# Attention and two expert layers in one kernel: the early weight chunks and the coefficients get other places in the order of issue

## The chip, the cores and the metric

The kernel runs on one core of one Trainium2 chip. The metric is the device time of one launch in microseconds; lower is better.

## The reference

```python
scores = scale * q @ k.T                       # 4 batches, 8 heads, 576 rows, 64 wide
scores = where(scores >= max(scores) - tau, scores, -1e9)
x = softmax(scores) @ v                        # then heads side by side: 2304 x 512
h = x @ w_in                                   # 512 x 2048, float64 weights
P = a[0] + a[1]*h + a[2]*h**2 + a[3]*h**3
Q = 1 + abs(b[0])*abs(h) + abs(b[1])*h**2
x = (P / (Q + 1e-6)) @ w_out                   # 2048 x 512, float64 weights
e = argmax(x @ w_gate, axis=1)                 # top-1 of 8 experts
out[rows of e] = gate_w * sigmoid(x @ w_output_gate)[e] * (relu(x @ w1[e]) @ w2[e])
```

## The kernel before

Every instruction is issued by a hand-written order; each engine takes its own in that order and waits on semaphores.

*Attention.* `attention` runs 144 steps, 18 to a group of four heads, N = 144. A step makes one block of scores on TensorE (`emit_s`, L356). VectorE takes the row minimum (L367) and masks (L380), ScalarE takes the exponential (L368) and writes the high half of the probabilities (L384), GpSimd the low half (L386, L392). Every two steps SP issues a DMA transpose of that pair (L394), out of a ring of four buffers. The product with v (`emit_pv`, L414) follows twelve steps later (LAG). After six such products VectorE normalises: a reciprocal and a multiplication (`emit_x`, L424, L425). The next product writes the same PSUM tile and waits for it. `emit_xt` turns normalised rows into xT (TensorE L206, ScalarE L445), `emit_xlo` makes the low half (VectorE L451). Pieces of the next group's queries and keys and of v are put into `plan`, by step.

*The second stage beside it.* `moe1` is a generator. The loop enters it once per step in the last 33 steps (`next(tail)` where `i >= N - PRE`), so its slot t stands at step 112 + t. Its first entry issues the loads of the coefficients a and b on SP (L678, L679); `coefficients` (L681) then negates and takes absolute values on VectorE and ScalarE. Slots hold lists of functions (`at`, `run`).

*Weight chunks.* w_in and w_out come as 32 raw chunks of 512 KB in the order of `STREAM`, (0, n) for w_in and (1, n) for w_out, through five buffers. `IN_LOAD` gives the slots of the first seven loads (L610); later ones are issued when a chunk has been decoded. A chunk is decoded from its float64 bits by ScalarE (`exponent`, L622) and three VectorE passes (`bits` L619, `merge` L625, `sign` L629). The first two chunks have their passes at the slots of `EARLY_STEPS`, the next six at `FIRST_AT`. `sum_in` (ScalarE, L801) sums absolute values; per two chunks `red_in` adds the rows on TensorE (L810) in a `tp` tile, `clamp_red` and `scale_in` (L635 to L654) make a power of two on VectorE, `split_in` splits the scaled chunk into two halves on ScalarE and GpSimd (L847, L848, L852).

*Chunks of the second stage.* From slot START on, `emit_in(c)` multiplies one chunk of w_in with three tiles of rows (L947). At odd c it issues, for that pair, three ScalarE passes (L970 to L972), a GpSimd product (L973) and two VectorE passes (L975, L976); for the pair before, three more VectorE passes (L961 to L963), whose result feeds `emit_out` (L1016), five chunks behind. Slot 34 is cut into three (`HALVES`): the second row sum, its scale and the first of its splits come between the last products of the attention, which are issued after the loop, one part at a time, between entries of the generator.

Of the kernel before, what the change touches and what calls it, by code (L numbers as in the profile page):

```python
# [49 lines left out]
MAG_BUFS = 4  # L50
MAG2_BUFS = 6
PART_BUFS = 3
PRE = 32
END = 37
START = 33
G_LAG = 5
FILL = (0, 0, 9, 0, 0)
IN_LOAD = (0, 3, 13, 17, 21, 32, 32)
STREAM = ((0, 0), (0, 1), (0, 2), (0, 3), (1, 0), (1, 1), (1, 2), (1, 3), (0, 4), (0, 5), (0, 6), (0, 7), (1, 4), (1, 5), (1, 6), (1, 7), (0, 8), (0, 9), (0, 10), (0, 11), (1, 8), (1, 9), (0, 12), (0, 13), (1, 10), (1, 11), (0, 14), (0, 15), (1, 12), (1, 13), (1, 14), (1, 15))
EARLY_STEPS = ((9, 11, 13), (15, 17, 19))  # L60
EARLY_SUM = 20
FIRST_AT = (13, 19, 32, 33, 35, 37, 37, 38)
SHIFT_LEAD = 3
SLOT_LEAD = (2, 1)
SECOND_SUM = 34
HALVES = (34,)
DEC_AT = 39
DEC_EVERY = 1.6


# [65 lines left out]
def attention(nc, tc, q, k, v, tau, xT, vs, ident, tail, bank):  # L136
# [260 lines left out]
    def emit_pv(i):  # L397
        g, hh, t = step(i)
        par = g % 2
        pt = pairs[i // 2]  # L400
        k = UT * (i % 2)
        if i % 6 == 0:

            nc.tensor.matmul(xflat, tiny[:, 0:P], tiny[:, P:], start=True, stop=False)
        b_hi, b_lo = (k + 5, k) if hh else (k, k + 5)
        parts = ((0, P, 0),) if t < 4 else ((0, 64, 0), (64, 64, 1)) if t == 4 else ((0, P, 1),)
        for po, m, bb in parts:
            rows = [4 * bb + (j + 2 * hh) % 4 for j in range(4)]
            seq = [(b_hi + j, vv, r) for j, r in enumerate(rows) for vv in (vh, vl)]
            seq += [(k + 4, vv, 8 + bb) for vv in (vh, vl)]  # L410
            seq += [(b_lo + j, vh, r) for j, r in enumerate(rows)]
            x = xps[po:po + m, i % 6, :]
            for n, (blk, vv, j) in enumerate(seq):
                nc.tensor.matmul(  # L414
                    x, pt[:, blk, po:po + m], vv[:, par, hh, j, :], start=False, stop=(i % 6 == 5 and n == 13))
# [3 lines left out]
    def emit_x(n):  # L419
        g, m = divmod(n, 3)  # L420
        if m == 0:
            xfs[g] = x_p.tile([P, GT, D], F32, tag="xf", name="xf")
        rs = sm.tile([P, 6, 1], F32, tag="rinv", name="rinv")
        nc.vector.reciprocal(rs, xps[:, :, D:D1])  # L424
        nc.vector.tensor_tensor(  # L425
            xfs[g][:, 6 * m:6 * m + 6], xps[:, :, 0:D], rs.to_broadcast([P, 6, D]), op=ALU.mult)
# [8 lines left out]
    def emit_xt(g, tg, k=None, what=None):  # L435
        if (g, tg) == (NG - 1, 2):
            tp = xflat[:, 0:3 * P].rearrange("p (a b) -> p a b", b=P)
        else:
            tp = ps_x.tile([P, 4, P], F32, tag="tp", name="tp")
        if what:  # L440
            piece_t(k, what, tp=tp, n=3)
        for t in range(3):
            for hh in range(2):
                turn(tp[:, t], hh, xfs[g][:, UT * hh + 3 * tg + t], ident)
        nc.scalar.activation(x_rows(g, tg, 0), tp[:, 0:3], AF.Copy)  # L445
        if what:
            piece_out(k, what)
        xts[g, tg] = tp
# [42 lines left out]
    def at(step, f, *a):  # L491
        plan.setdefault(step, []).append((f, a))
# [43 lines left out]
    pre = {6 * n + 6 + LAG: n for n in range(N // 6 - 2)}  # L536
    for g in range(NG):
        for tg in range(3):
            s = min((g + 1) * GT + PLAN["xt"][tg], N)
            if g == NG - 1:  # L540
                continue
            w = (g + 2, (("kt",), ("qt", 0), ("qt", 1))[tg]) if g + 2 < NG else ()
            at(s, emit_xt, g, tg, *w)
            at(min(s + 1, N), emit_xlo, g, tg)
    emit_s(0)
    for i in range(N + 1):
        if i + 1 < N:
# [21 lines left out]
    next(tail)  # L569
    for i in range(N - LAG, N - 6):  # L570
        emit_pv(i)
    next(tail)
    emit_x(N // 6 - 2)
    for i in range(N - 6, N - 4):
        emit_pv(i)
    next(tail)
    for i in range(N - 4, N - 2):
        emit_pv(i)
    emit_xt(NG - 1, 0)
    emit_xlo(NG - 1, 0)  # L580
    next(tail)
    for i in range(N - 2, N):
        emit_pv(i)
    emit_x(N // 6 - 1)
# [83 lines left out]
def moe1(nc, tc, xT, vs, w_in, w_out, a, bb, w_gate, w_ogate, gates, ident, yd, part, L, consts, keep, side, early_bank):  # L668
# [43 lines left out]
    def at(slot, f, *args):  # L712
        hooks.setdefault(max(slot, 0), []).append((f, args))
# [143 lines left out]
        nc.scalar.activation(h, f, AF.Copy)  # L857
        nc.gpsimd.tensor_tensor(l, f, h.bitcast(F32), op=ALU.subtract)  # L858

    at(1, coefficients)  # L860
    end = decode_at()
    for key in STREAM:
        t = end[key]
        if key in STREAM[:2]:
            for x, f in zip(EARLY_STEPS[STREAM.index(key)], step_parts(key)):
                steps.setdefault(x, []).append(f)
            t = EARLY_STEPS[STREAM.index(key)][0]
        else:
            steps.setdefault(t, []).append(lambda key=key: step(key))
        at(t - SLOT_LEAD[late(key)], exponent, key)  # L870
        if late(key) and key[0]:
            at(t - SHIFT_LEAD, last_bits, key)
    n = 0
    for m in GROUPS:
        if n < 2 * m:
            for i in range(n, n + m):
                at(end[0, i] + (n == 0), sum_in, i)
            t = SECOND_SUM if n else EARLY_SUM + 1
            at(t + 0.5, red_in, n, m, True)
            at(t + 0.75, clamp_red, n, m)  # L880
            at(t + 0.75, scale_in, n, m)
            for i in range(m):
                at(t + (0.8, 1)[i] if n else t + 2 + 2 * i, split_in, n + i)
            at(t + 1, factors_in, n, m)
        else:
            for i in range(n, n + m):
                at(end[0, i] + 1, sum_in, i)
            t = max(end[0, i] for i in range(n, n + m)) + 1
            at(t + 1, red_in, n, m)
            at(t + SC_LAG, scale_in, n, m)  # L890
            at(t + SC_LAG, factors_in, n, m)
            for i in range(m):
                at(t + IN_LAG + i * SPLIT2, split_in, n + i)
        n += m
# [40 lines left out]
    def emit_in(c, fill):  # L935

        p, odd = divmod(c, 2)
        ops, late = [], []
        if c < len(chunks):
            j, fc, r = chunks[c]  # L940
            t0 = TR * r
            if not odd:
                hps[p] = h_tile()
            hb = hps[p][:, odd]
            parts = [(0, k, lo) for k in range(4) for lo in range(2)] + [(1, k, 0) for k in range(4)]
            for i, (w, k, lo) in enumerate(parts):
                nc.tensor.matmul(  # L947
                    hb[:, 0:n], w_cols(w, fc)[:, k], xT[:, k, t0:t0 + TR, lo, :],
                    start=(i == 0), stop=(i == 11))
            if spare:  # L950
                first, last = spare.pop(0)(hb[:, n:DM])
                if first:
                    first()
                late.append(last)
        if odd:
            if p - 1 in st:
                q = p - 1
                t, s = st.pop(q)
                x = hps.pop(q)[:, :, 0:n]
                ops += [  # L960
                    lambda: stt(t, t, one, x, op0=ALU.add, op1=ALU.mult),  # L961
                    lambda: stt(x, t, 2.0, x, op0=ALU.subtract, op1=ALU.mult),
                    lambda: (stt(s, s, na0, x, op0=ALU.add, op1=ALU.mult), emit_g(q, s)),  # L963
                ]
            if c < len(chunks):

                hp = hps[p][:, :, 0:n]
                c1, c2, ca1, ca3 = (cvs[:, i, t0 // UT, fc - 1:fc] for i in range(4))
                ah, t1, s1 = buf("ah", 1), buf("t", 3), buf("s", 4)
                nc.scalar.activation(ah, hp, AF.Abs, scale=c1)  # L970
                nc.scalar.activation(s1, hp, AF.Identity, bias=na2, scale=ca3)
                nc.scalar.activation(t1, ah, AF.Identity, bias=b0, scale=b1)  # L972
                nc.gpsimd.tensor_tensor(t1, t1, ah, op=ALU.mult)  # L973
                ops += [
                    lambda: stt(s1, s1, c2, hp, op0=ALU.mult, op1=ALU.mult),  # L975
                    lambda: stt(s1, s1, ca1, hp, op0=ALU.add, op1=ALU.mult),  # L976
                ]
                st[p] = t1, s1
        elif p - 1 in st:

            x, t = hps[p - 1][:, :, 0:n], st[p - 1][0]
            nc.scalar.activation(x, t, AF.Ln, bias=one)  # L982
            nc.scalar.activation(x, x, AF.Exp, scale=-1.0)
        ops += late
        fill = list(fill)
        for f, k in itertools.zip_longest(ops, FILL):
            if f:
                f()
            for _ in range(min(k or 0, len(fill))):
                fill.pop(0)()  # L990
        for f in fill:
            f()
# [896 lines left out]
```

## Time and profile before

| | us |
|---|---|
| median of 3 runs | 1029.98 (1028.72 to 1033.62) |
| profiled execution | 1033.16 |
| its span, first to last instruction | 1031.4 |
| TensorE busy | 934.7 (91%) |
| VectorE busy | 797.6 (77%) |
| ScalarE busy | 680.4 (66%) |
| GpSimd busy | 542.5 (53%) |

The attention loop fills the first 312 us or so, the second stage with the expert layers the rest. In the rows PE is TensorE and PEld its weight loads, DVE is VectorE, ACT ScalarE, POOL GpSimd, SP SyncE, and SPq SP's issue of DMAs. Times are counted from the span's start. A bracket at the end of a row tells how long the engine stood idle before it, and what ended that.

### The profile page before, as it was taken

What the parts mean: (1) busy time and instruction counts of PE and PEld (TensorE: products, weight loads), DVE (VectorE), ACT (ScalarE), POOL (GpSimd) and SP (SyncE); (2) the same over time, 40 slices, a digit from 0 to 9 for tenths busy, and PEclk for the clock granted to TensorE, in tenths of its full rate; (3) what the DMA queues carried; (4) which work ended last, traced back from release to release, by engine and by line L of the source; (5) the groups of instructions that cost most, each with busy time, mean ns of one, the idle gap of its engine ahead of it and who ended that gap; (6) DMA issues with size and microseconds to landing.
All of it is one profiled execution on the core that took longest, in us unless ns stands there. A gap on an engine that the chain in (4) does not pass through costs nothing. (4 is left out here: it accounts for less than half of the span.)

```text
span 1031.4 us, 20730 instructions
## 1 busy us (share of the span) xinstructions
PE 934.7 (91%) x7899; PEld 685.4 (66%) x7899; DVE 797.6 (77%) x1337; ACT 680.4 (66%) x1006; POOL 542.5 (53%) x540
## 2 busy tenths in 40 slices
PE   8898899996977799999899999998798999999996
PEld 5565566664655465666566666665477899999995
DVE  5897799985996897888767878898983896656552
ACT  5888888885885687788756666665462555545552
POOL 2687689885793569687964444444241131111120
PEclk9999999998998899999999999999899999999998
DMA  9999999998998233223003213032123011111340
GB/s 211 175 203 204 197 190 188 185 198 158 163 194 181 81 106 131 82 92 113 1 1 82 72 31 93 2 92 89 55 52 131 23 52 52 42 42 42 108 138 24
DMA packets 234188, 110.26 MB, mean 107 GB/s; under 512 B 196832, under 2 KB 221408, under 8 KB 234080
## 3 DMA queue, kind: packets, MB, share of 16 engines
q1 hardware_dynamic: 230816, 98.89, 44.3%
q0 software_dynamic: 3120, 9.96, 3.0%
q8 instruction: 64, 1.05, 0.4%
q14 instruction: 44, 0.36, 0.1%
q10 hardware_dynamic: 144, 0.00, 0.0%
HBM read 82.61 MB, written 13.63 MB: 93 GB/s over the span
## 5 line engine op out<-in xcount | busy, mean ns | idle before, releaser
L386 POOL TENSOR_TENSOR php<-e,php 128x512 f16<-128x512 f32 x144 | 166.5, 1160 | 73.8 <-ACT php L384 73.5
L973 POOL TENSOR_TENSOR t<-t,ah 128x768 f32<-128x768 f32 x48 | 88.3, 1839 | 176.3 <-ACT t L972 169.8
L947 PE MATMUL h<-xT,wih 128*128 128x384 f16 x768 | 145.0, 333 | 34.5 <-DVE s L963 22.4
L947 PEld LDWEIGHTS <-wih 128*128 128x128 f16 x768 | 68.8, 99 | 99.4 <-DVE s L963 28.2
L368 ACT ACTIVATE e<-s,mn 128x576 f32<-128x576 f32 x144 | 107.1, 744 | 32.9 <-DVE mn L367 29.7
L1016 PE MATMUL acc<-woh,gh 128*128 128x512 f32 x288 | 126.2, 438 | 2.9 <-ACT woh L857 1.6
L414 PEld LDWEIGHTS <-pt 128*128 128x128 f16 (+1 forms) x2240 | 79.7, 102 | 67.7 <-issue 55.4
L356 PE MATMUL s<-kt,qT 64*128 64x256 f32 (+3 forms) x640 | 116.1, 452 | 8.3 <-DVE mn L373 7.6
L380 DVE SCALAR_TENSOR_TENSOR e<-s,mn,e 128x576 f32<-128x576 f32 x144 | 116.3, 808 | 5.1 <-ACT e L368 5.1
L1716 POOL DMA_INDIRECT out_dram<-os,sidx x19 | 24.3, 1277 | 181.7 <-ACT os L1715 150.9
L1016 PE MATMUL acc<-wol,gh 128*128 128x512 f32 x288 | 114.3, 397 | 1.2 <-POOL wol L858 1.1
L1016 PE MATMUL acc<-woh,gl 128*128 128x512 f32 x288 | 114.4, 397 | 0.8 <-POOL gl L998 0.5
L367 DVE TENSOR_REDUCE mn<-s 128x1 f32<-128x576 f32 x144 | 107.7, 748 | 9.3 <-PE s L356 9.1
L384 ACT ACTIVATE php<-e 128x576 f16<-128x576 f32 x144 | 98.6, 685 | 5.5 <-DMA pt<-php 2.7
L998 POOL TENSOR_TENSOR gl<-s,gh 128x768 fp32r<-128x768 f32 x48 | 91.2, 1900 | 9.9 <-ACT gh L997 4.9
L414 PE MATMUL xps<-vs__112,pt 128*128 128x65 f16 (+1 forms) x2240 | 94.1, 197 | 0.0
L982 ACT ACTIVATE h<-t,co 128x768 f32<-128x768 f32 x48 | 43.5, 906 | 64.8 <-POOL t L973 26.4
L947 PE MATMUL h<-xT,wil 128*128 128x384 f16 x384 | 79.4, 330 | 1.1 <-POOL wil L852 1.1
L970 ACT ACTIVATE ah<-h,cvs 128x768 f32<-128x768 f32 x48 | 43.3, 903 | 47.9 <-PE h L947 43.4
L961 DVE SCALAR_TENSOR_TENSOR t<-t,co,h 128x768 f32<-128x768 f32 x48 | 48.5, 1010 | 30.9 <-POOL gl L998 23.8
L1649 DVE TENSOR_TENSOR wol<-xT,woh 128x1024 fp32r<-128x1024 f32 x45 | 56.8, 1271 | 13.5 <-ACT woh L1648 12.7
L1016 PEld LDWEIGHTS acc<-woh,gh 128*128 128x128 f32 x288 | 54.8, 190 | 17.5 <-ACT part L1033 2.1
(390 smaller groups left out, 2323.2 us busy)
## 6 DMA issues: line engine op xcount, KB each, us to landing
xT<-in_moe_w_dram SPq DMA_DIRECT2D x80, 512.0 KB
raw<-in_moe_w_in_dram SPq DMA_DIRECT2D x16, 512.0 KB
raw<-in_moe_w_out_dram SPq DMA_DIRECT2D x16, 512.0 KB
yd<-y SPq DMA_DIRECT2D x18, 256.0 KB
raw<-in_k_dram SPq DMA_DIRECT2D x16, 256.0 KB
raw<-in_q_dram SPq DMA_DIRECT2D x16, 256.0 KB
xT<-in_v_dram SPq DMA_DIRECT2D x8, 512.0 KB
part<-part SPq DMA_DIRECT2D x15, 256.0 KB
```

The costliest lines, as they stand in the source:

```text
L356: nc.tensor.matmul(ps[po:po + m, o:o + n], qT[r, g % 2, hh, t, po:po + m], KT[g][r, bb, c:c + n], start=True, stop=True)
L367: nc.vector.tensor_reduce(mn[:, n:n + 1], st[i], axis=AX.X, op=ALU.min)
L368: nc.scalar.activation(e[:, n], st[i], AF.Exp, bias=mn[:, n:n + 1], scale=-1.0)
L380: nc.vector.scalar_tensor_tensor(e[:, n], st.pop(i), mn[:, 2 + n:3 + n], e[:, n], op0=ALU.is_le, op1=ALU.mult)
L384: nc.scalar.activation(hi, e[:, n], AF.Copy)
L386: nc.gpsimd.tensor_tensor(lo[:, b:b + 512], e[:, n, a:a + 512], hi[:, a:a + 512], op=ALU.subtract)
L414: nc.tensor.matmul(x, pt[:, blk, po:po + m], vv[:, par, hh, j, :], start=False, stop=(i % 6 == 5 and n == 13))
L947: nc.tensor.matmul(hb[:, 0:n], w_cols(w, fc)[:, k], xT[:, k, t0:t0 + TR, lo, :], start=(i == 0), stop=(i == 11))
L973: nc.gpsimd.tensor_tensor(t1, t1, ah, op=ALU.mult)
L998: nc.gpsimd.tensor_tensor(gl, s, gh.bitcast(F32), op=ALU.subtract)
L1016: nc.tensor.matmul(acc[r, i], g[:, i * P:(i + 1) * P], w, start=first and m == 0, stop=last and m == 2)
L1649: (self.nc.gpsimd if pool else self.nc.vector).tensor_tensor(cut(lo), src, cut(hi).bitcast(F32), op=ALU.subtract)
```

## The change

The generator is entered 20 steps sooner, from step 92 on. Its slots from START on move by the same 20, so that most of the work keeps its step. What is moved: `coefficients` runs in slot 30 (step 122), its loads are issued at step 92. The first two raw chunks are loaded at steps 100 and 104 (before: 112 and 115) and decoded at 111, 113, 117 and 119, 123, 125 (before: 121, 123, 125 and 127, 129, 131); the first row sum moves from step 133 to 127, with its scale and splits. The exponents of the next chunks are listed one by one (three of them 3 to 4 steps sooner, three a slot later), and the fourth chunk's `sum_in` is one slot later, behind `emit_in(1)`. Turning the rows of the group before the last is moved from step 144 to 142. After the loop the normalisation of the six products is issued ahead of the second part of the cut slot, and chunk 1's two VectorE passes are issued in that part, behind it. Four products stand together before the third part, and the turn of the last group's first rows behind it.

```diff
-PRE = 32
-END = 37
-START = 33
+PRE = 52
+END = 57
+START = 53
-IN_LOAD = (0, 3, 13, 17, 21, 32, 32)
+IN_LOAD = (8, 12, 33, 37, 41, 52, 52)
+COEFFICIENTS = 30
-EARLY_STEPS = ((9, 11, 13), (15, 17, 19))
-EARLY_SUM = 20
-FIRST_AT = (13, 19, 32, 33, 35, 37, 37, 38)
+EARLY_STEPS = ((19, 21, 25), (27, 31, 33))
+EARLY_SUM = 35
+FIRST_AT = (25, 33, 52, 53, 55, 57, 57, 58)
+FIRST_EXPONENTS = (17, 25, 46, 48, 50, 56, 56, 57)
-SLOT_LEAD = (2, 1)
-SECOND_SUM = 34
-HALVES = (34,)
-DEC_AT = 39
+SECOND_SUM = 54
+HALVES = (54,)
+DEC_AT = 59
...
@@ attention
-            s = min((g + 1) * GT + PLAN["xt"][tg], N)
+            s = min((g + 1) * GT + PLAN["xt"][tg], N - 2)
-            at(min(s + 1, N), emit_xlo, g, tg)
+            at(s + 1, emit_xlo, g, tg)
...
     for i in range(N - LAG, N - 6):
         emit_pv(i)
+    emit_x(N // 6 - 2)
     next(tail)
-    emit_x(N // 6 - 2)
-    for i in range(N - 6, N - 4):
+    for i in range(N - 6, N - 2):
         emit_pv(i)
     next(tail)
-    for i in range(N - 4, N - 2):
-        emit_pv(i)
     emit_xt(NG - 1, 0)
+    next(tail)
     emit_xlo(NG - 1, 0)
-    next(tail)
     for i in range(N - 2, N):
         emit_pv(i)
...
@@ moe1
-    at(1, coefficients)
+    at(COEFFICIENTS, coefficients)
...
-            t = EARLY_STEPS[STREAM.index(key)][0]
-        at(t - SLOT_LEAD[late(key)], exponent, key)
+        at(t - 1 if late(key) else FIRST_EXPONENTS[STREAM.index(key)], exponent, key)
...
-                at(end[0, i] + (n == 0), sum_in, i)
-            t = SECOND_SUM if n else EARLY_SUM + 1
+                at(end[0, i] + (i != 2), sum_in, i)
+            t = SECOND_SUM if n else EARLY_SUM
...
         ops += late
+        if c == 1:
+            at(HALVES[0] + 0.5, lambda ops=ops: [f() for f in ops])
+            ops = []
```

## Rows read from the trace of the kernel before

**Rows 1.** Busy time by stretch: length, each engine's busy time (instructions), clock, DMA, GB/s.
```profile
...
195.31:229.26 33.95, 33.42 (x509) 22.82 (x509) 31.12 (x63) 29.52 (x52) 29.51 (x38) 1.00 1.09 199
...
277.00:302.00 25.00, 20.20 (x301) 13.23 (x300) 24.31 (x57) 20.11 (x36) 22.69 (x30) 1.00 1.07 201
...
```

**Rows 2.** Timeline, VectorE, 195 to 335: start, us, instruction, [idle before <- releaser].
```profile
...
195.91 0.20 DVE L424 RECIPROCAL rinv<-xps 128x6 f32<-128x6 f32 x1 [0.83 <-PE xps L414]
...
229.87 0.20 DVE L424 RECIPROCAL rinv<-xps 128x6 f32<-128x6 f32 x1 [0.83 <-PE xps L414]
...
249.89 0.19 DVE L424 RECIPROCAL rinv<-xps 128x6 f32<-128x6 f32 x1
...
263.83 0.20 DVE L424 RECIPROCAL rinv<-xps 128x6 f32<-128x6 f32 x1 [0.56 <-PE xps L414]
...
288.83 0.18 DVE L424 RECIPROCAL rinv<-xps 128x6 f32<-128x6 f32 x1
...
300.60 0.18 DVE L424 RECIPROCAL rinv<-xps 128x6 f32<-128x6 f32 x1
...
```

**Rows 3.** Timeline of all engines, 240 to 262.
```profile
...
247.03 0.57 SPq L678 DMA_DIRECT2D co<-in_moe_a_dram  x1
...
249.80 0.17 DVE L682 TENSOR_SCALAR co<-co 128x4 f32<-128x4 f32 x1 [9.41 <-DMA co<-in_moe_a_dram]
...
250.73 0.48 PE L404 MATMUL xps<-tiny 128*128 128x390 bf16 x1 [9.10 <-DVE xf L425]
...
```

**Rows 4.** Busy time by stretch, where the granted clock is low.
```profile
...
247.00:251.00 4.00, 0.27 (x1) 0.10 (x1) 1.17 (x6) 0.19 (x1) 0.00 (x0) 0.50 0.67 152
251.00:258.00 7.00, 7.00 (x83) 5.17 (x83) 4.85 (x10) 4.54 (x8) 4.22 (x6) 0.61 0.44 93
...
323.00:328.00 5.00, 4.75 (x75) 4.33 (x76) 0.98 (x10) 1.35 (x2) 1.36 (x2) 0.50 0.71 264
...
```

**Rows 5.** Timeline, TensorE, 305 to 365.
```profile
...
318.78 0.38 PE L810 MATMUL tp<-tot,co 128*128 128x2 f32 x2 [1.04 <-ACT wih L801]
323.25 0.48 PE L404 MATMUL xps<-tiny 128*128 128x390 bf16 x1 [4.08 <-DVE xf L425]
...
333.30 1.47 PE L947 MATMUL h<-xT,wih 128*128 128x384 f16 x8 [1.69 <-ACT wih L848]
...
```

**Rows 6.** Timeline, VectorE, 305 to 365.
```profile
...
320.44 1.01 DVE L975 SCALAR_TENSOR_TENSOR s<-s,cvs,h 128x768 f32<-128x768 f32 x1 [2.46 <-ACT s L971]
...
322.42 0.19 DVE L424 RECIPROCAL rinv<-xps 128x6 f32<-128x6 f32 x1
...
337.34 1.01 DVE L975 SCALAR_TENSOR_TENSOR s<-s,cvs,h 128x768 f32<-128x768 f32 x1 [1.94 <-ACT s L971]
...
```

**Rows 7.** Timeline, SP's queue, 150 to 330.
```profile
...
221.85 15.91 SPq L394 DMA_TRANSPOSE pt<-php  x5
...
259.15 20.20 SPq L394 DMA_TRANSPOSE pt<-php  x5
...
```

**Rows 8.** Line 384 (ScalarE): what its idle time waited for; us, times.
```profile
...
  DMA pt<-php: 2.7, 3
...
```

**Rows 9.** Timeline, VectorE: sign pass in the loop, after it, among chunks.
```profile
...
275.47 0.95 DVE L629 SCALAR_TENSOR_TENSOR mag<-raw,mag 128x512 int32<-128x512 int32 x1
...
315.49 0.69 DVE L629 SCALAR_TENSOR_TENSOR mag<-raw,mag 128x512 int32<-128x512 int32 x1
...
345.68 2.19 DVE L629 SCALAR_TENSOR_TENSOR mag<-raw,mag 128x512 int32<-128x512 int32 x1
...
```

**Rows 10.** Timeline of all engines, 286 to 304: the first scale.
```profile
...
293.22 0.16 DVE L635 TENSOR_SCALAR t<-tp 128x2 f32<-128x2 f32 x1 [0.59 <-PE tp L810]
...
```

**Rows 11.** Timeline, ScalarE, 305 to 365.
```profile
...
316.22 0.63 ACT L801 ACTIVATE wih<-mag 128x512 f16<-128x512 f32 x1 [2.80 <-DVE mag L629]
...
318.01 0.63 ACT L801 ACTIVATE wih<-mag 128x512 f16<-128x512 f32 x1 [0.48 <-DVE mag L629]
...
323.68 0.72 ACT L847 ACTIVATE mag<-mag,sc 128x512 f32<-128x512 f32 x1 [2.36 <-DVE sc L653]
...
```

## The prediction

> **What bounds the kernel now.** I read the busy time by stretch first, then the normalisation passes in order, then the idle times, engine by engine. In the attention loop eighteen steps take 33.95 us, and TensorE is busy for 33.42 of them, VectorE for 31.12 [rows 1]: the loop goes at TensorE's pace, with 2.8 us of VectorE left over. Near its end this turns: in the 25 us from 277 on VectorE is busy for 24.31 and TensorE for 20.20 [rows 1].
>
> One reciprocal per six steps (L424) is the loop's clock. From 195.91 to 229.87 three such intervals take 33.96, 11.32 each. The next takes 249.89 - 229.87 = 20.02, the one after 13.94, the two together after that 25.00, and the last 11.77 [rows 2]. So 8.7 + 2.6 + 2.4 + 0.4 us above the loop's own pace lie here, all after step 112, where the second stage's generator is entered for the first time.
>
> The first excess is a wait. `coefficients` runs one step after the generator has issued the loads of the coefficients. SP is in order and issues them only at 247.03, behind transposes; VectorE has by then stood for most of its 9.41 us, TensorE for its 9.10, which is put down to VectorE's normalisation [rows 3]. Of VectorE's wait only 249.80 - 247.03 = 2.8 us is the load itself; the rest is SP's queue. The second excess is the granted clock: 0.50 in 247 to 251 and 0.61 on average in 251 to 258, in which TensorE is busy all 7.00 us [rows 4]; that is its lower level of 1.2 GHz for most of the stretch, after TensorE had stood still. The third is the six decode passes of the first two weight chunks, the fourth the split of those weights.
>
> At the end of the loop there is another hole. TensorE is through with a group of products at 318.78 - 1.04 = 317.74 and starts the next at 323.25, having waited 4.08 of it for VectorE's normalisation [rows 5]. That one (L424 at 322.42) stands behind chunk 1's two passes of 1.01, the first of which waited 2.46 for ScalarE [rows 6]. The clock falls again: 0.50 from 323 to 328 [rows 4].
>
> **The change, part by part.** The profiled execution took 1033.16 us, 1.76 more than its span; the median of the runs is 1029.98, 3.2 less. I sum against the profiled one and take the gain off the median.
>
> *Coefficients.* The loads go out at step 92, their readers come at step 122, some 57 us later at 33.95 / 18 = 1.89 a step. The wait goes. Nothing else was late during it, since the transposes that SP had in hand are used twelve steps after they are made. Gain 8.7 by the reciprocals, 9.4 by the idle row: I take 8.7, which is in step time. The four small instructions themselves (0.17 for the longest, [rows 3]) stay.
>
> *The clock after it.* With no standstill TensorE keeps its full clock: 2.6, at least 1.0 if part of this is the pipeline filling again. I take 2.6.
>
> *First weights sooner.* Two loads of 512 KB leave SP at steps 100 and 104 instead of 112 and 115; the other early loads keep their place against the end of the loop. What queues behind them are transposes. SP needs 15.91 / 5 = 3.18 us per transpose in the plain loop and 20.20 / 5 = 4.04 in the stretch with a weight load [rows 7], while a pair of steps gives 3.77. So a load costs from nothing (there is room in the queue) to 20.20 - 15.91 = 4.3 us, two of them 8.6. A late transpose shows first at ScalarE, which writes over a buffer four transposes old: it waited for one 3 times in the whole loop, for 2.7 us [rows 8]. That is the nearest row, so I take a loss of 0.5.
>
> *Decode passes.* The same six, at steps 111 to 125 instead of 121 to 131. They cost 2.4 us of step time where they stand. Most go to where TensorE sets the pace and VectorE has 2.8 us in eighteen steps to spare, out of a stretch which VectorE sets. The best case is that they become free, a gain of 2.4. The worst is that they take their full 0.95 each [rows 9], 5.7 against 2.4, a loss of 3.3. I take a gain of 0.6.
>
> What speaks against the early place is GpSimd, which is busy for 29.51 of 33.95 there [rows 1]. A sign pass (L629) takes 0.69 at 315.49, 0.95 in the loop, and 2.19 at 345.68, where GpSimd had a long pass running [rows 9]. The Trainium skill (SBUF — State Buffer, Who interferes with whom) has it that a VectorE instruction with two SBUF inputs is held for the whole of a GpSimd instruction that reads SBUF. By that rule each of the four such passes could lose what the longest row lost, 2.19 - 0.69 = 1.5, or 6.0 together, and the gain would end 6.6 lower; by the loop's row it is 0.26 each. The rows of the loop agree with the small figure, since GpSimd was running there too.
>
> *First scale sooner.* The row-sum matmul goes from step 133 to step 127. VectorE waited 0.59 for it [rows 10]. In step 127 its PSUM tile is still being copied out by ScalarE (the last piece of the queries), so TensorE waits a little longer: 0 to 1.2, I take a loss of 0.6. The two splits move with it, out of the VectorE-bound stretch; their engines have room: 0.
>
> *End of the loop.* Normalisation now stands ahead of chunk 1's passes. VectorE is free at 320.44 - 2.46 = 317.98 [rows 6], so it comes at about 318.0 instead of 322.42. TensorE does not follow at once: the second row-sum matmul (L810) stands ahead of its next product, and needs the fourth chunk's sum, which ran at 318.01 [rows 11] and now is queued behind chunk 1's three ScalarE passes. ScalarE had idle time of 2.80 and 0.48 just there [rows 11]. If the passes fit in it, that matmul runs at about 319.2, and TensorE goes on 4.0 us sooner; if they only start at 318.0 (the sum and two of them filled 318.01 to 320.44, the sum and three need some 3.5), it is 321.5 and TensorE goes on 1.5 sooner. With the exponents gone to earlier steps I take 3.8. A gap of 1.5 in place of 5.1 should leave the clock up: 75 matmuls took 4.75 at half clock [rows 4], at most 2.4 of it comes back, I take 2.0. The split of the third chunk waits 2.36 for its scale and the product of the fourth waits 1.69 for its split [rows 5, 11]; both chains start sooner with the scale, 0 to 1.7, I take 0.7. The transposed rows moved from step 144 to 142 are the same work. Together 6.5, from 1.5 to 8.1.
>
> *Sum.* 8.7 + 2.6 - 0.5 + 0.6 - 0.6 + 6.5 = 17.3. After 337 no engine waits for a load and the chunks depend only on one another, so the shift runs to the end. The profiled execution becomes about 1015.9, the median 1029.98 - 17.3 = 1012.7.
>
> **Rivals.** *The end of the loop gains nothing* (the sum behind chunk 1's passes takes the place of the wait that went): for it speaks that TensorE is in order and the row-sum matmul stands ahead of the products; against it ScalarE's idle time [rows 11]. Gain 17.3 - 6.5 = 10.8, time 1019.2. Chance 0.17.
>
> *The transposes fall behind*: the two loads cost 5 us, against the 0.5 assumed. For it: 4.04 per transpose is more than the 3.77 that the steps give [rows 7]. Against it: ScalarE's 2.7 us in all [rows 8]. Gain 12.8, time 1017.2. Chance 0.10. [...]
>
> *More comes back*: the decode passes are free (2.4, not 0.6) and the end of the loop gives its upper bound (8.1, not 6.5): 3.4 more, time 1009.3. For it speaks VectorE's room [rows 1], against it GpSimd's share of the loop. Chance 0.07.
>
> *The wait moves to the first exponents, and the kernel gets slower.* ScalarE reads the first two raw chunks at steps 109 and 117, 9 and 13 steps after their loads are queued on SP. If each load stands there as the coefficients' did, ScalarE waits 9.4 at both, and with 2.6 of clock after each that is 24: 1012.7 + 24 = 1036.7. It decides from the point where a load lands more than nine steps, 17 us, after step 100. Against it: the coefficients needed 2.8 from issue to reader, and about 10 with SP's queue. Chance 0.04. One wait alone gives 1024.7: 0.03 more, no change that can be told.
>
> **Numbers.** The forecast has the remaining 0.59, by itself 1008.5 to 1017. The range 1007 to 1020 takes in the first two rivals, most of the third, and leaves the last out. A measurement of this kernel can tell about 0.5%, 5 us, from no change: faster 0.93, same 0.03, slower 0.04.
>
> **What would show it.** VectorE has no idle row of more than 2 us between 229 and 311, and the granted clock stays at 1.00 there; the reciprocals from step 108 on are 11 to 12.5 us apart. ScalarE's wait for transposes stays under 4 us in total and it has no wait for a raw chunk. The reciprocal now at 322.42 comes some 17.5 us behind the one now at 300.60, not 21.8 [rows 2, 6], TensorE's wait there is under 2 us, and chunk 3's pass (L975, at 337.34 now, [rows 6]) comes some 17 us sooner. The prediction is wrong if any idle of 5 us or more stands anew in the loop, if the clock falls after its end as before, or if the stages after 337 take longer than they did.

## The result, and the profile after

| | median, us | kernel before in the same rounds: median; ratio [95% interval] |
|---|---|---|
| changed kernel, first runs (4) | 1017.58 | 1031.02; ratio 0.9877 [0.9831, 0.9923] |
| again (6) | 1018.37 | 1030.24; 0.9878 [0.9853, 0.9903] |
| a third time (5) | 1015.73 | 1031.25; 0.9858 [0.9837, 0.9879] |

By the ratios the change makes the kernel 12.6 to 14.6 us faster; 17.3 was forecast. Over all 15 runs the median is 1016.5 against the 1012.7 forecast. The profiled execution after took 1022.82 (span 1020.8), the longest of the 15.

Lines of attention stand one further down in the changed kernel (L424 is L425), those of the second stage one or two further up (L810 is L809, L975 is L973). First the reciprocals on VectorE, then chunk 3's pass (timeline; start, duration):

```profile
229.95 0.20 DVE L425 RECIPROCAL rinv<-xps 128x6 f32<-128x6 f32 x1 [0.83 <-PE xps L415]
243.67 0.18 DVE L425 RECIPROCAL rinv<-xps 128x6 f32<-128x6 f32 x1
255.72 0.18 DVE L425 RECIPROCAL rinv<-xps 128x6 f32<-128x6 f32 x1
268.09 0.18 DVE L425 RECIPROCAL rinv<-xps 128x6 f32<-128x6 f32 x1
281.94 0.18 DVE L425 RECIPROCAL rinv<-xps 128x6 f32<-128x6 f32 x1
292.15 0.20 DVE L425 RECIPROCAL rinv<-xps 128x6 f32<-128x6 f32 x1
...
309.76 0.19 DVE L425 RECIPROCAL rinv<-xps 128x6 f32<-128x6 f32 x1
324.44 1.01 DVE L973 SCALAR_TENSOR_TENSOR s<-s,cvs,h 128x768 f32<-128x768 f32 x1 [0.82 <-ACT s L969]
```

Up to 229.95 both run alike [rows 2]. From 229.87 to 300.60 the kernel before needs 70.73, from 229.95 to 292.15 this one 62.20: 8.5 sooner at the loop's end. The reciprocal of 322.42 comes at 309.76, chunk 3's pass of 337.34 at 324.44 [rows 6], 12.9 sooner. The 9.41 and the 9.10 of [rows 3] are gone. The loop has new, small waits: ScalarE for the transposes, and TensorE, VectorE and ScalarE around the first row sum (timeline, all engines):

```profile
235.03 0.68 ACT L385 ACTIVATE php<-e 128x576 f16<-128x576 f32 x1 [1.34 <-DMA pt<-php]
...
243.24 0.68 ACT L385 ACTIVATE php<-e 128x576 f16<-128x576 f32 x1 [0.80 <-DMA pt<-php]
...
272.69 0.57 ACT L253 COPY qT<-tp 128x512 f32<-128x512 f32 x1
...
273.31 0.38 PE L809 MATMUL tp<-tot,co 128*128 128x2 f32 x2 [1.33 <-ACT qT L253]
...
273.73 0.16 DVE L634 TENSOR_SCALAR t<-tp 128x2 f32<-128x2 f32 x1 [1.84 <-PE tp L809]
...
275.42 0.74 ACT L369 ACTIVATE e<-s,mn 128x576 f32<-128x576 f32 x1 [2.16 <-DVE mn L368]
```

The end of the loop, all engines: the second row sum (L809) waits 2.52 for the fourth sum (L800 at 311.06), which ScalarE has behind chunk 1's three passes; the next product (L405) no longer waits for the normalisation, which is done by then [rows 5, 11].

```profile
304.49 2.78 POOL L387 TENSOR_TENSOR php<-e,php 128x512 f16<-128x512 f32 x2 [1.03 <-ACT php L385]
304.72 1.53 DVE L624 SCALAR_TENSOR_TENSOR mag<-raw 128x512 int32<-128x512 int32 x1
...
306.29 1.53 DVE L628 SCALAR_TENSOR_TENSOR mag<-raw,mag 128x512 int32<-128x512 int32 x1
...
307.23 0.88 POOL L393 TENSOR_TENSOR php<-e,php 128x128 f16<-128x128 f32 x1
...
307.85 0.63 ACT L800 ACTIVATE wih<-mag 128x512 f16<-128x512 f32 x1 [2.78 <-DVE mag L628]
...
308.43 0.69 DVE L624 SCALAR_TENSOR_TENSOR mag<-raw 128x512 int32<-128x512 int32 x1
308.48 0.88 ACT L968 ACTIVATE ah<-h,cvs 128x768 f32<-128x768 f32 x1
...
310.14 1.02 ACT L970 ACTIVATE t<-ah,co 128x768 f32<-128x768 f32 x1
...
311.06 0.62 ACT L800 ACTIVATE wih<-mag 128x512 f16<-128x512 f32 x1
...
311.82 0.59 PE L809 MATMUL tp<-tot,co 128*128 128x2 f32 x2 [2.52 <-ACT wih L800]
312.27 0.49 PE L405 MATMUL xps<-tiny 128*128 128x390 bf16 x1
```

Busy time by stretch, with the granted clock in the column ahead of the last two; after, then before for the two late stretches:

```profile
229.90:249.90 20.00, 17.28 (x261) 11.85 (x262) 18.22 (x36) 15.11 (x26) 16.67 (x23) 1.00 1.10 211
...
274.00:278.00 4.00, 4.00 (x42) 2.67 (x38) 3.69 (x15) 2.03 (x5) 1.20 (x3) 0.57 1.01 237
...
312.00:320.00 8.00, 7.82 (x125) 6.36 (x125) 3.74 (x15) 4.34 (x7) 2.73 (x2) 0.80 0.99 306
...
490.00:520.00 30.00, 24.26 (x114) 15.75 (x115) 18.63 (x31) 18.52 (x25) 22.12 (x20) 0.89 0.00 1
560.00:600.00 40.00, 37.48 (x212) 25.56 (x211) 30.45 (x44) 24.40 (x29) 18.16 (x18) 0.96 0.22 60
```

```profile
490.00:520.00 30.00, 24.42 (x119) 15.24 (x118) 22.76 (x35) 22.37 (x31) 27.94 (x23) 0.94 0.00 1
560.00:600.00 40.00, 36.77 (x211) 24.70 (x210) 33.28 (x48) 25.99 (x33) 18.25 (x24) 1.00 0.26 67
```

The clock is 1.00 where the stall was [rows 4]. In this execution it is 0.57 in 4 us behind the first row sum, which the forecast had not foreseen; in the two others of the changed kernel (e7 and e11, below) it stays at 1.00 there. It is 0.80 behind the loop, and lower than before at about 500 and 575, where the change issues nothing new.

### The profile page after: what moved, and what is told of

It is laid out like the page before. It is cut to its first block, busy times and chain, and to the rows that moved or that the text cites. A ratio compares the mean times of both kernels' runs of the same rounds, so it can differ in the third digit from the quotient of the medians.

```text
span 1020.8 us, 20731 instructions
## 1 busy us (share of the span) xinstructions
PE 938.0 (92%) x7899; PEld 687.2 (67%) x7899; DVE 797.8 (78%) x1337; ACT 680.4 (67%) x1006; POOL 542.8 (53%) x540
## 4 chain that ended last, share of the span: by engine, by line
PE 48%; DVE 20%; POOL 11%; issue 10%; ACT 8%; DMA 2%; SPq 0%; POOLq 0%; ACTq 0%; DVEq 0%
PE h L1690 10%; PE o L1707 9%; PE h L945 6%; PE acc L1017 6%; PE s L357 5%; PE tp L207 5%; PE xps L415 4%; POOL t L971 3%; DVE e L381 3%; POOL gl L999 2%; DVE t L959 2%; DVE h L960 2%; POOL raw L616 2%; POOL wol L857 1%; DMA pt<-php 1%
```

## The experiments

Executions differ by -1.3 to +5.0 us already ahead of step 92, before the changed part begins. In the last two columns this difference is taken off. *Loop*: how much sooner than in the profile of before step 143 begins on VectorE. *Chunks*: the same for the two VectorE passes of the third pair of chunks (chunk 5). What lies between is the end of the loop.

| profiled execution | loop | chunks | median, ratio |
|---|---|---|---|
| changed kernel | 8.5 | 14.5 | 1017.58, 0.9877 |
| changed again (e7) | 10.5 | 17.3 | 1018.37, 0.9878 |
| changed, third (e11) | 10.5 | 17.9 | 1015.73, 0.9858 |
| e1 coefficients only | 8.8 | 9.1 | 1021.76, 0.9910 |
| e2 weights at old steps | 11.2 | 18.6 | 1017.40, 0.9863 |
| e3 row sum later | 11.3 | 18.5 | 1014.63, 0.9840 |
| e10 the same again | 10.1 | 16.0 | 1019.41, 0.9877 |
| e4 old end of loop | 10.5 | 12.2 | 1022.55, 0.9925 |
| e5 second sum behind | 10.1 | 17.8 | 1017.87, 0.9876 |
| e6 last low half on VectorE | 11.3 | 17.3 | one run, 1024.93 |
| e8 new end alone | 2.3 | 3.8 | 1030.86, 0.9998 |
| e9 new end with exponents | 2.1 | 8.1 | 1027.92, 0.9964 |
| e12 before again | 2.0 | 2.4 | 1030.08, 0.9991 |

**e1.** Before, with one edit.

```diff
-    at(1, coefficients)
+    at(10, coefficients)
```

> The kernel before, with the coefficients read at slot 10 (step 122) instead of slot 1; everything else stays. My theory (the wait and the low clock after it are a plain loss of step time): the idle rows of 9.4, 9.4 and 9.1 us go, the reciprocal now at 249.89 comes at about 241.2 and the one now at 300.60 at 289.3, 11.3 sooner; the time falls by 11 us, to about 1020. Rival (the queue of transposes catches up during the wait, so part of it comes back as a wait of ScalarE for transposes): the reciprocal at 300.60 comes only 6 to 9 us sooner.

The reciprocal of 249.89 came 9.0 sooner and that of 263.83 11.5: stall and clock are worth 8.7 + 2.6, as read. Then 1.8 was lost again at step 126 and 0.9 more by step 130, so that the loop ends 8.8 sooner, within the rival's 6 to 9. The loads still leave SP at step 112, and SP's queue shows the transposes behind them. ScalarE's next write into their ring then stood 2.48; the profile names a VectorE instruction for it, but ScalarE's queue stood until the semaphore of a transpose was complete, at 263.03:

```profile
247.43 0.57 SPq L678 DMA_DIRECT2D co<-in_moe_a_dram  x1
248.52 1.59 SPq L610 DMA_DIRECT2D raw<-in_moe_w_in_dram  x1
250.27 3.59 SPq L394 DMA_TRANSPOSE pt<-php  x1
253.90 0.58 SPq L610 DMA_DIRECT2D raw<-in_moe_w_in_dram  x1
...
263.11 0.68 ACT L384 ACTIVATE php<-e 128x576 f16<-128x576 f32 x1 [2.48 <-DVE mn L373]
```

This execution is not a usual one, though. It is the longest of the seven of e1, 2.6 above their median, and SP's queue was late in it before the programs differ: a load of queries left at 209.3 (counted as in the profile of before) where it left at 207.4 in e2. By its ratio e1 gains 9.3, between 6.1 and 12.4.

**e2.** The changed kernel with the first two weights and the first row sum at their old steps.

```diff
-IN_LOAD = (8, 12, 33, 37, 41, 52, 52)
+IN_LOAD = (20, 23, 33, 37, 41, 52, 52)
-EARLY_STEPS = ((19, 21, 25), (27, 31, 33))
-EARLY_SUM = 35
-FIRST_AT = (25, 33, 52, 53, 55, 57, 57, 58)
-FIRST_EXPONENTS = (17, 25, 46, 48, 50, 56, 56, 57)
+EARLY_STEPS = ((29, 31, 33), (35, 37, 39))
+EARLY_SUM = 41
+FIRST_AT = (33, 39, 52, 53, 55, 57, 57, 58)
+FIRST_EXPONENTS = (27, 33, 46, 48, 50, 56, 56, 57)
```

> The changed kernel, with the first two weight chunks at their old steps: loads at steps 112 and 115, decode at 121 to 131, row sum at step 133. In the changed kernel the last reciprocal of the loop comes 8.0 us sooner than before, where I had worked out 11 to 12. My theory (3 to 4 us are lost to two things of the early place: the loads stand ahead of transposes, and the row sum waits for its PSUM tile): the last reciprocal of the loop comes at about 299.5, 3.3 sooner than in the changed kernel, the row-sum wait of VectorE is 0.6 again, and the time is 3 us below the changed kernel's. Rival (the early decode is free and the wait was simply worth less): it comes at 302.8 as in the changed kernel or later, and the time is the same or higher.

The gain of 11.46 is there at step 118 and is held to step 140. Against e1 that is 2.7 more at that step. In the loop up to there the two programs differ only in when the coefficients' loads leave SP (step 92 here), but since e1's queue was late before that, how much of the 2.7 is the place of the loads is not shown. Against the changed kernel (10.5 at best) it is 0.7 to 0.9 more: decoding the first weights sooner costs the loop a little. The median is not the 3 us lower that was expected.

**e3 and e10.** The changed kernel with the first row sum in step 130, once, and again in the same rounds as e11.

```diff
-EARLY_SUM = 35
+EARLY_SUM = 38
```

> The changed kernel, with the first row sum three steps later (step 130, where the PSUM tile is free), scale and splits behind it. My theory: VectorE's wait of 1.84 us for the row sum and TensorE's of 1.33 for the copy shrink to 0.6 or less, step 128 costs about 2.1 us less, the loop ends 1.3 to 2 us sooner, the time falls by as much. Rival (VectorE sets the pace here, and the wait only took the place of its own work): the loop ends at the same time within 0.5 us.

> The changed kernel with the first row sum three steps later (slot 38 in place of 35), word for word as it was run before (1014.6 then). Theory (the row sum in step 127 costs 2 to 2.8 us and nothing else in the change depends on its place): the step that lost 2.1 us gains 0.6 again, and the median is 2.5 to 4 us under that of the changed kernel in the same call, near 1014.6. Rival (the first measurement was a low draw): less than 1 us under it.

The step that grew by 2.14 gained 0.6 here, both times; TensorE and VectorE no longer wait for each other (e10, timeline):

```profile
274.50 0.36 PE L809 MATMUL tp<-tot,co 128*128 128x2 f32 x2
...
274.90 0.16 DVE L634 TENSOR_SCALAR t<-tp 128x2 f32<-128x2 f32 x1
...
276.57 0.74 ACT L369 ACTIVATE e<-s,mn 128x576 f32<-128x576 f32 x1 [1.02 <-DVE mn L368]
```

But from step 128 to 143 the changed kernel gains 3.0 (e7, e11) and e10 loses 0.2, e3 gains 1.0. At the loop's end the later place is worth -0.4 to 0.8, and over the runs nothing: ten of the later sum have a mean of 1017.4, fifteen of the changed kernel 1017.6. In the same rounds e10 is 3.7 above e11. The first result of e3 was a low draw; the rival was right.

**e4.** The changed kernel with the end of the loop, chunk 1's passes, the fourth sum and step 144's transposed rows as before.

```diff
-        if c == 1:
-            at(HALVES[0] + 0.5, lambda ops=ops: [f() for f in ops])
-            ops = []
...
-                at(end[0, i] + (i != 2), sum_in, i)
+                at(end[0, i] + (n == 0), sum_in, i)
```

> The changed kernel with the end of the loop issued as before: the normalisation behind the second part of the cut slot, chunk 1's two VectorE passes in their old place, the turn of the group before the last at step 144, the fourth chunk's sum a slot sooner. My theory (5.9 us of the gain come from here): the loop ends as in the changed kernel, the first reciprocal after it comes 4 to 5 us later than there (at about 314), TensorE waits 4 us for it, the clock falls behind it for some 7 us, and the time is 5 to 6 us above the changed kernel's. Rival (the row sum behind chunk 1's ScalarE passes holds TensorE as long as the normalisation did): the time is within 2 us of the changed kernel's.

Between loop and chunks 1.6 are gained, against 5.9 to 7.3 in the three profiles of the changed kernel. The first reciprocal behind the loop comes 5.2 later than in the first of them, counted from step 143, and the median is 5.0 above the first of the changed kernel: the theory held. TensorE stands as before:

```profile
312.70 0.48 PE L405 MATMUL xps<-tiny 128*128 128x390 bf16 x1 [4.08 <-DVE xf L426]
```

**e8 and e9.** Before with the new end alone (the edits that e4 takes back), and with the exponents of the third to the eighth chunk at the changed kernel's slots as well.

```diff
+LATER_EXPONENTS = (26, 28, 30, 36, 36, 37)
...
-        at(t - SLOT_LEAD[late(key)], exponent, key)
+        k = STREAM.index(key)
+        at(LATER_EXPONENTS[k - 2] if 2 <= k < 8 else t - SLOT_LEAD[late(key)], exponent, key)
```

> The kernel before with the new end of the loop alone: normalisation ahead of chunk 1's VectorE passes, these behind the cut, the fourth chunk's sum a slot later, the turn of the group before the last at step 142. Coefficients, loads and exponents stay where they were, so the wait of 9.4 us is in it. My theory (4 to 6 us of the gain belong to the end of the loop and add up with the rest): the time falls by 4 to 5.5 us, to about 1025.5, and the clock stays up after the loop. Rival (it pays only together with the earlier exponents, which free ScalarE there): it falls by less than 2.5 us.

> The kernel before with the new end of the loop (as in the run of the new end alone), and beside it the six exponents of the weights that are decoded around the end of the loop converted at the changed kernel's slots (26, 28, 30, 36, 36, 37) in place of two steps ahead of each decode. The coefficients, the first two weights and the first row sum stay where they were. Either half alone gave 1.5 us or less at the chunks behind the loop. Theory (the two need each other: the new end puts ScalarE's exponents ahead of the fourth sum, the old exponents keep the old order's sums back): chunk 2 and those behind it come 5 to 7 us sooner than before, after the loop's own difference is taken off; the median 1024 to 1026 by a time before of 1030.3. Rival (the end gains only when the loop itself ends sooner, because GpSimd's and the transposes' work lies otherwise then): at most 2 us, the median 1028 to 1031.

The new end alone gains 1.5 at the chunks and nothing by the median, so its rival was right; with the exponents it gains 6.0. In both, the first reciprocal behind the loop comes 6.6 sooner than before (the loop's 2.1 to 2.3 included); the difference comes behind it. An exponent, the row sum and the clock, e8 and then e9:

```profile
313.73 0.68 ACT L620 ACTIVATE raw<-raw 128x512 f32<-128x512 f32 x1
...
317.64 0.58 PE L808 MATMUL tp<-tot,co 128*128 128x2 f32 x2 [3.17 <-ACT wih L799]
```

```profile
316.00:326.00 10.00, 8.36 (x102) 6.83 (x102) 5.18 (x15) 4.90 (x9) 3.49 (x2) 0.66 0.93 300
```

```profile
318.36 0.53 PE L809 MATMUL tp<-tot,co 128*128 128x2 f32 x2 [2.45 <-ACT wih L800]
```

```profile
316.00:326.00 10.00, 7.64 (x119) 6.31 (x120) 5.95 (x18) 6.13 (x10) 3.49 (x2) 0.83 1.11 299
```

With the exponent (313.73) ahead of the passes and the fourth sum, TensorE stands 3.17 and not 2.45. It also has more of the ten microseconds at its lower level after it; that the longer gap did this is not shown, since behind the same 2.45 in e2 the clock stayed at 1.00. The 5 to 7 of e9's theory is met at chunk 5 (chunk 3's pass gains 4.5), its median is not: 3.3 below before where 4 to 6 were expected. Against e12 the chunks of e9 are 5.7 sooner, and 1.5 of that went again at about 505 in the profiled execution, which leaves 4.2.

**e5.** e3 with the second row sum behind the four products that it stood ahead of.

```diff
-            at(t + 0.5, red_in, n, m, True)
+            at(t + (0.75 if n else 0.5), red_in, n, m, True)
```

> The kernel of the run before with the first row sum at step 130, and the second row-sum matmul (L809) moved behind the four products that follow it. There TensorE stood idle 2.62 us before that matmul, until ScalarE had summed the fourth chunk, though the normalisation was ready 1.5 us sooner. My theory (in the changed kernel the row sum, in order ahead of the products, is what holds TensorE after the loop): the idle time falls to about 1.2 us, the products run 1.5 us sooner, the third chunk's matmuls start 0.5 to 1 us sooner and what follows with them; time 1013.5 to 1014.5. Rival (scale and split set the pace behind it, and they come later now): chunk 3 starts no sooner, time 1015 or above.

```profile
312.81 0.36 PE L809 MATMUL tp<-tot,co 128*128 128x2 f32 x2
...
315.22 1.47 PE L945 MATMUL h<-xT,wih 128*128 128x384 f16 x8 [0.92 <-ACT wih L847]
```

TensorE's wait ahead of L809 is gone, and the next chunk waits 0.92 for its split instead. Counted from step 143 chunk 3's pass comes 0.5 sooner than in e3, but the ratio, 0.9876, is that of e10, 0.9877: nothing is gained that the runs can tell.

**e6.** e3 with the low half of the last step's probabilities made on VectorE.

```diff
-        nc.gpsimd.tensor_tensor(lo[:, b:b + 512], e[:, n, a:a + 512], hi[:, a:a + 512], op=ALU.subtract)
+        low = nc.vector if i == N - 1 else nc.gpsimd
+        low.tensor_tensor(lo[:, b:b + 512], e[:, n, a:a + 512], hi[:, a:a + 512], op=ALU.subtract)
...
-            nc.gpsimd.tensor_tensor(y, w, z, op=ALU.subtract)
+            low.tensor_tensor(y, w, z, op=ALU.subtract)
```

> The kernel with the first row sum at step 130, the last step's low half of the probabilities (two passes) made by VectorE instead of GpSimd. In that kernel the first decode after the loop took 1.25, 1.53 and 0.80 us where the next one took 0.42, 0.69 and 0.69, and GpSimd ran until 305.2 beside the first. My theory (VectorE's passes are held by GpSimd's): with GpSimd idle after about 303.2 the merge pass takes 0.7 to 0.8 and the sign pass 0.7, 0.8 us less in all, and VectorE's own two added passes cost about 1. Rival (they are slow because ScalarE's exponent writes the same buffer late, or for some other reason of their own): the merge still takes 1.5 us.

```profile
306.21 1.16 POOL L388 TENSOR_TENSOR php<-e,php 128x512 f16<-128x512 f32 x1 [0.77 <-ACT php L385]
```

```profile
308.50 0.69 DVE L625 SCALAR_TENSOR_TENSOR mag<-raw 128x512 int32<-128x512 int32 x1
309.23 0.69 DVE L629 SCALAR_TENSOR_TENSOR mag<-raw,mag 128x512 int32<-128x512 int32 x1
```

With GpSimd through at 307.4 the passes that took 1.53 take 0.69. VectorE has the low half to do in return (0.69 and 0.28), and the end of the loop gains 6.0, where e3's gains 7.2. The clock fell behind the loop here and did not in e3, so this one execution does not tell what the edit is worth.

**e7 and e11.** The changed kernel, unaltered.

> The changed kernel once more, word for word. In its first trace ScalarE waited 2.5 us in three places for transposes, and step 112 was 2.05 us longer than before; with the row sum later, or the old end of the loop, it did not wait and step 112 was 0.7 us longer, though the two early loads stood in the same place. My theory (this wait comes and goes from one execution to another, so it explains less than 1.5 us of the median): the trace has less than 1 us of it, step 128 is again 2.1 us longer, and the median is 1016 to 1018. Rival (the loads in front of the transposes are a lasting cost): again 2 us or more of that wait and 2 us at step 112.

> The changed kernel, unaltered, so that the later row sum is compared with it on the same chip in the same rounds. Both theories: 1017.5 to 1018.5, the step with the row sum 2.1 us longer than before, and a wait of 0 to 1.4 us for the transposes behind the first decode pass.

Step 112 is 0.69 longer than before in both (2.05 in the first profile, where the waits for transposes add up to 2.5), step 128 2.14 longer in all three. In the first profile SP's queue was late already: the first of the two early loads left it at 226.7, counted as in the profile of before, and at 224.0 and 224.6 in e7 and e11. The medians miss their ranges, by 0.4 above (e7) and by 1.8 below (e11). The chunks are 17.3 and 17.9 sooner, where 17.3 was forecast for the whole kernel; e11 then loses 1.5 at about 505.

**e12.** Before, unaltered.

> The kernel before, unaltered, for a second profiled execution of it. In the profile that the prediction was made from VectorE waited 9.41 us for the coefficients; in two kernels that have that wait in the same place it was 7.60 and 7.57, and the loop 2.3 us shorter for it. Theory (the profiled execution of before was a long one, by its stall, so the forecast took 8.7 us off a median that has only some 6.5 to lose): the wait is 7.4 to 8.2 here, the reciprocal behind it comes about 18.2 us behind the one ahead of it, not 20.0, and the execution takes 1029 to 1032. Rival (9.4 is the usual wait, and the two others were short by their changed end): 9.2 to 9.6, and 20.0 between the two reciprocals. The median against itself: within 0.25% of 1.

```profile
231.17 0.20 DVE L424 RECIPROCAL rinv<-xps 128x6 f32<-128x6 f32 x1 [0.83 <-PE xps L414]
...
249.85 0.17 DVE L682 TENSOR_SCALAR co<-co 128x4 f32<-128x4 f32 x1 [8.17 <-DMA co<-in_moe_a_dram]
249.95 0.19 DVE L424 RECIPROCAL rinv<-xps 128x6 f32<-128x6 f32 x1
```

Here the wait is 8.17, and 7.60 and 7.57 in e8 and e9, against 9.41 in the profile that the forecast was read from [rows 3]. The two reciprocals stand 18.8 apart, between the 18.2 and the 20.0 of the two theories; the loop is 2.0 shorter, behind the stall of e8 and e9 it is 2.3. The stall in the profile before was the longest of four. The difference is SP's queue. Counted from the same start, the load leaves it at 247.03 in that profile, at 245.8 here (the row below, less the 1.30 that this execution is late), and at 245.2 in e8 and e9; the stalls differ by the same 1.2 and 1.8. Why the queue is later in one execution than in another is not shown.

```profile
247.09 0.57 SPq L678 DMA_DIRECT2D co<-in_moe_a_dram  x1
```

## Why the prediction was right, and where it was off

*Coefficients and clock, 8.7 + 2.6.* The mechanism was right, and for the profiled execution the size too (e1, e2: 11.46). The step that failed is the one that took this sum off the median: in three other executions the stall was shorter and the loop with it, by 2.0 to 2.3, so the usual one has some 9.2 to lose, not 11.3. The place of the loads was priced at nothing, and the runs do not show that it is worth more: e1, which leaves them where they were, gains 9.3 by its ratio, and the 2.7 that it loses in its profile is that of an execution whose queue was late before.

*Loads of the first weights, -0.5.* Between 0 and 1.4 at step 112, by the execution: 0.69 of the growth there comes in every execution with the early decode passes, the rest of the 2.05 in the first profile alone. The rival of 5 did not come.

*Decode passes, +0.6, and first row sum, -0.6.* Together -0.7 to -0.9 (e2 against e7 and e11). The row sum was mis-sized where it stands: 2.14 and not 0.6, since VectorE waits too (1.84) and ScalarE behind it (2.16). But 3.0 comes back in the steps behind it, which no longer have that work. Of the four moved passes that merge and set signs one was long and two were shorter: 1.31, 0.68, 0.75 and 0.95, in place of 0.87, 0.87, 0.95 and 0.94. Their sum is 3.69 against 3.63, so the loss of 6.0 that was weighed did not come (VectorE, after):

```profile
242.43 1.31 DVE L624 SCALAR_TENSOR_TENSOR mag<-raw 128x512 int32<-128x512 int32 x1
...
251.42 0.75 DVE L628 SCALAR_TENSOR_TENSOR mag<-raw,mag 128x512 int32<-128x512 int32 x1
```

*End of the loop, +6.5.* Measured 5.9, 6.8 and 7.3. That the size was met is in part luck, since its parts came otherwise. Counted from step 143, TensorE goes on 2.5, 3.6 and 2.7 sooner (3.8 was taken; the bound of 1.5 should have been 1.75, from 321.5 to 323.25), and still stands 2.52, 1.67 and 2.56 (under 2 was foreseen). The clock was 0.80 and 0.79 on average in 312 to 320 in the first profile and e7; only in e11 it stayed up (e11: TensorE, and the 8 us behind):

```profile
308.51 0.38 PE L809 MATMUL tp<-tot,co 128*128 128x2 f32 x2 [2.56 <-ACT wih L800]
```

```profile
309.00:317.00 8.00, 7.42 (x131) 5.66 (x130) 5.04 (x18) 4.69 (x7) 3.69 (x4) 1.00 1.00 312
```

In the profiles with new end and exponents where it stayed up (e2, e3, e5, e11) the end gains 7.2 to 7.7, in the others 5.9 to 6.8. And 1.5 of the gain comes between chunks 3 and 5, which e4 has too, with the old end. What the forecast missed is on what the gain hangs. "With the exponents gone to earlier steps" stood in it as a half sentence; without them the new end is worth 1.5 (e8), and without the new end they are worth 1.6 (e4). So the rival *the end of the loop gains nothing* is close to what either half gives.

*"The shift runs to the end."* Not wholly. In all profiles of the changed kernel and its variants, 1.5 to 1.8 went again at about 505 or 575, in the first of them and in e5 at both; in the first the granted clock was 0.89 and 0.96 there, where before had 0.94 and 1.00. Why it falls there is not shown. Of the two that put the new end into the kernel before, e8 lost as much at both places and e9 at 505; e1 and e12 did not. That the stages after 337 take longer was named as a sign of being wrong, and this step was wrong by that much. At about 740, e4, e5 and e7 gained 3.7. At the last instruction the three profiles of the changed kernel are 10.7, 16.4 and 16.3 sooner than the first of before, and e12 is 2.9 sooner.

*The sum.* 17.3 less about 2.1 (the stall of the usual execution) less about 1.6 (the late clock) is 13.6; the ratios give 12.6 to 14.6. From the profiles, the 17.3 and 17.9 of e7 and e11 at the chunks, less the 2.4 of e12 and less 1.6, are 13.3 and 13.9. The first profile, 8.5 for the loop and 14.5 for the chunks, is of an execution with late transposes, and the longest of its kernel.

*The signs.* Of those that were named, VectorE's idle rows, the wait for transposes and the reciprocal behind the loop (17.6 behind the one ahead of it) came as foreseen. The clock stayed at 1.00 in the loop in e7 and e11, not in the first profile. The reciprocals in the loop were 10.2 to 13.9 apart, not 11 to 12.5, and chunk 3's pass came 12.9, 15.8 and 16.4 sooner, not 17.

*The rivals.* No wait moved to the first exponents; the transposes were waited for by 2.5 in all at most; the 3.4 more of the third did not come back.

*The rule that was weighed.* Two passes behind the loop took 1.53 beside GpSimd's low half, 0.69 without it (e6), and GpSimd's own short pass 0.88 beside one, 0.43 alone. The Trainium skill (SBUF — State Buffer, Who interferes with whom) says that a VectorE instruction with two SBUF inputs contends with a GpSimd instruction that reads SBUF: this trace agrees, 1.53 against 0.69; in the loop the same lines took 0.68 to 1.31, so that not every pass is held. In e7 VectorE's first such pass behind the loop began 0.16 ahead of GpSimd's: it took 0.69, and GpSimd's took 1.55 in place of 1.16. What this does to the kernel's time is not shown by e6's one execution.

## What to carry to other kernels

A small load is as late as the queue that it is issued in: put its reader far enough behind it. That alone gave 9.3 here by the ratio (e1); whether moving the issue ahead of the crowded stretch adds to it is not shown. Read the size of a stall from more than one execution before it is taken off a median, since this one was 7.6 to 9.4. At a place where several engines hand over in turn, two reorderings may be worth 1.5 us each and 6 together: ask for each what stands next in line, and try them together.

## What the runs showed of the hardware

Behind nearly the same gap at the same place the granted clock fell in some executions and not in others. TensorE stood 2.52 ahead of 311.82, and the clock was 0.80 on average from 312 to 320; it stood 2.56 there in e11, and the clock stayed at 1.00. What decides it is not shown. SP's queue does not run alike from one execution to the next: the same load left it 1.8 us later in one than in another, and its reader stood 1.8 us longer (9.41 and 7.57). Executions that have the same work up to step 92 reach it up to 6 us apart (-1.3 to +5.0), which is half of what the change gains: single profiles have to be laid on each other at a common instruction before their steps are compared.
